# A sparse attention kernel with a mixture of depths: three kinds of small VectorE operations put behind a maximum, ScalarE's copies of the softmax sums left out, and one tile's gate product two maxima later

## The chip, the core and the metric

The kernel runs on one core of a Trainium2 chip. The core has five engines that run their own instruction streams side by side and wait for each other through semaphores: TensorE (PE in the profile; PEld are its weight loads), VectorE (DVE), ScalarE (ACT), GpSimd (POOL) and SyncE (SP), which here only starts DMAs. The metric is the device time of one execution in microseconds, as a median over runs.

## The reference

Two blocks, one after the other. `B, H, S, D` = 8, 8, 576, 64.

```python
scores = scale * np.matmul(q, k.transpose(0, 1, 3, 2))
kth = np.partition(scores, -32, axis=-1)[..., -32:-31]
scores = np.where(scores >= kth, scores, -1e9)
attn = np.exp(scores - np.max(scores, axis=-1, keepdims=True))
attn = attn / (np.sum(attn, axis=-1, keepdims=True) + 1e-09)
x = np.matmul(attn, v)                      # heads side by side: (B, S, 512)

gates = np.einsum('bsd,d->bs', x, w_gate)
out = x.copy()
for b in range(B):
    top = np.argpartition(-gates[b], 128)[:128]
    ye = np.maximum(x[b, top] @ w1, 0.0) @ w2
    out[b, top] = x[b, top] + ye / (1 + np.exp(-gates[b, top]))[:, None]
```

Each row of 576 scores keeps its 32 largest. Each batch then sends its 128 tokens with the largest gates through two matrix products.

## The kernel before

**Tiles and units.** The 576 query rows of a batch are four full tiles of 128 rows and a fifth of 64. A unit is two heads of a full tile (or four heads of the short one), so that a batch has 4 x 4 + 2 = 18 units and the whole run 144. A loop over `n` takes the units through a pipeline: in iteration `n` the scores of unit `n+1` are multiplied and copied to SBUF (`sc`), unit `n` gets a bound for its 32nd largest score, unit `n-1` is split at the bound, unit `n-2` gets its exact 32nd largest score (`kth_of`), unit `n-3` is masked and unit `n-4` is transposed, exponentiated and multiplied with `v`. All engines issue in the order in which the program is written.

**VectorE's share of a unit.** `find_bound`: for each of two rows of heads seven maxima over a seventh of the scores each (`cand<-sc`, 14 in a unit; one MAX8 instruction gives the eight largest), then rounds of maxima and replacements on these candidates. `find_kth`: two long maxima (`next<-y`), the last big instructions of a unit. Between these stand small ones. `find_bound` empties a list `vector_late` ahead of the second seven maxima; and `amid_late` holds the gate product of one tile with the number of the maximum in front of which it goes in the second seven.

**GpSimd's share.** For each unit two products (`y<-sc,sides`), a short `fill` of `y`, and one half of the mask (`less<-sc,next`); for each tile of queries the division by the softmax sums (`x<-xs,rden`); besides this the choice of the mixture's rows and its gathers and scatters.

**A tile's end.** When the last unit of a tile of queries has been multiplied with `v`, ScalarE copies the result into `xs` (eight heads of 64 columns and one column with the sum). `keep_sums` copies the eight sums into the constant tile `sums`, adding 1e-9. In the next iteration `normalise` takes the reciprocal on VectorE (`rden<-sums`, from `vector_late`) and has GpSimd multiply (`x<-xs,rden`). One iteration later `gates` takes the product of `x` with the gate's weights on VectorE (`prod<-x,wg`, a two-input operation with an accumulator). In the second seven maxima it stands in front of the maximum 2 in the first, fourth and fifth tile, 4 in the second and third.

**The mixture of a batch** is a generator, whose steps `mix_at` places in units of the batch that follows. Of its small VectorE operations three kinds matter here:
- `add_up`, run from `after_kth` behind `find_kth`: `add_parts` sums up a place (`place<-places`), `keep_rows` makes the row index (`row_i<-place`), then `g` is limited from below, and an `Exp` of `g` is put into `late`, a list for ScalarE that is emptied once in each iteration.
- `squash`, from `vector_late`: `g` plus 1, and its reciprocal.
- `keep_least`, at the end of each batch: the least of all 32nd largest scores (`least<-next`), for a check at the end of the kernel.

At the end of the kernel a list of such checks is worked off (two of them on `sums`), and if one fails, a slow general path runs. The last units stand outside the loop, written out by hand, with `sums_of` for the last two tiles.

Of the kernel before, what the change touches and what calls it, by code (L numbers as in the profile page):

```python
# [49 lines left out]
def kernel(  # L50
# [91 lines left out]
    seen = const.tile([P, NS], FP32, name="seen")  # L142
    least = const.tile([P, B], FP32, name="least")
    bounded = const.tile([P, NS], FP32, name="bounded")
    sums = const.tile([P, B * NT, H], FP32, name="sums")
    nc.gpsimd.memset(sums, 1.0)

    MIDDLE = S - 2 * (TOP_K - 8) + 1
    steps_i = const.tile([P, 2, 8], I32, name="steps_i")
# [74 lines left out]

    kept, values_bank = [], [None]

    after_kth = []

    def flush_copies():
        while copies_late:  # L230
# [14 lines left out]

    def flush_all():
        flush_vector()
        flush()
        flush_pool()

# [293 lines left out]
    def find_bound(sc, bound):  # L544

        cand = wkpool.tile([P, 2, 8 * PARTS], FP32, name="cand")
        best = [stats.tile([P, 2, 8], FP32, name=f"best{r}") for r in range(2)]
        best.append(bound)
        for i in range(2):

            if i == 1:
                flush_vector()
            for u in range(PARTS):
                if i == 1 and amid_late and u == amid_late[0][0]:
                    amid_late.pop()[1]()
                dve.max(
                    cand[:, i, 8 * u : 8 * u + 8],
                    sc[:, i, u * S // PARTS : (u + 1) * S // PARTS],
                )


        parts = cand.rearrange("p i (u e) -> p i u e", u=PARTS)
        for r, e in enumerate((3, 7, 8)):
            for i in range(2):
                dve.max(best[r][:, i, :], parts[:, i, :, 0:e])
            if r < 2:
                for i in range(2):
                    dve.match_replace(
                        parts[:, i, :, 0:e],
                        best[r][:, i, :],  # L570
                        parts[:, i, :, 0:e],
                        LOWEST,
                    )
# [140 lines left out]
    def keep_values_of_two(t, g, av, xs):  # L714
# [7 lines left out]
        for i, (h, r) in enumerate(heads_of(t, g)[0]):  # L722
# [4 lines left out]
                in_=both[r : r + n, :].rearrange("p (g c) -> p g c", g=2),  # L727
            )

    def normalise(b, t, xs):  # L730
        n = R if t == J else P
        den = sums[0:n, b * NT + t, :]
        divide(n, xs, of_batch[b][0][0:n, t, :], den)

    def keep_sums(n, xs, den):
        act.activation(den, xs[0:n, :, D], AF.Copy, bias=1e-9)

    def divide(n, xs, x, den):
        rden = stats.tile([P, H], FP32, name="rden")
        dve.reciprocal(out=rden[0:n, :], in_=den)  # L740
        pool.tensor_tensor(
            x.rearrange("p (h d) -> p h d", h=H),
            xs[0:n, :, 0:D],
            rden[0:n, :].unsqueeze(2).to_broadcast([n, H, D]),
            ALU.mult,
        )

# [38 lines left out]
    def mixture(row0, pg, rank, exact=False, sign_sum=None):  # L786
# [107 lines left out]

        def add_up():
            add_parts(place, found)
            keep_rows(
                place,
                row_i,
                row0 if isinstance(row0, float) else row0[:, 0:1],  # L900
                float(done * S - 1),
            )
            dve.tensor_scalar_max(out=g, in0=place[:, 1:2], scalar1=-88.0)
            late.append(lambda: act.activation(g, g, AF.Exp, scale=-1.0))

        def squash():
            dve.tensor_scalar_add(out=g, in0=g, scalar1=1.0)
            dve.reciprocal(out=g, in_=g)

        kept.append(lambda: after_kth.append(add_up))  # L910
        if exact:
            for todo in (kept, after_kth):
                while todo:
                    todo.pop(0)()
        yield
# [126 lines left out]
    def gates(b, t):  # L1042
        dot_tile(t, *of_batch[b])
# [130 lines left out]
    def keep_least(b, bound, kth):  # L1174
        at = 2 * per_batch * b
        late.append(
            lambda: act.copy(
                out=bounded[:, at : at + 2 * per_batch].rearrange("p (n i) -> p n i", i=2),
                in_=bound,
            )  # L1180
        )
        dve.tensor_reduce(
            out=least[:, b : b + 1], in_=kth, axis=mybir.AxisListType.XY, op=ALU.min
        )

    def mask_of(n, on=None):
# [5 lines left out]
    for n in range(-1, N):  # L1192
# [35 lines left out]
            normalised = None  # L1228
        if gating is not None:

            amid_late.append((4 if gating[1] in (1, 2) else 2, lambda a=gating: gates(*a)))

# [47 lines left out]
        if is_unit(n - 4):  # L1282
            b4, t4, g4 = units[n - 4]
            values(t4, g4, pT, last, av, qkv[b4][2], 2 * DE * second)
            if n in place_steps:
                values_bank[0] = av
                next(mixtures[place_steps[n]])
                pieces[place_steps[n]] += 1
            if g4 == 0:
                xs = xpool.tile([P, H, DE], FP32, name="xs")  # L1290
                if t4 == 0:
                    x = xpool.tile([P, NT, HD], FP32, name="x")
                    pg = gates_of[b4 % 2]
                    of_batch[b4] = x, pg
            if second:
                keep_values_of_two(t4, g4 - 1, av, xs)
            if g4 == groups(t4) - 1:
                inverting = b4, t4, xs
                n4 = R if t4 == J else P
                keep_sums(n4, xs, sums[0:n4, b4 * NT + t4, :])  # L1300
            while kept:
                kept.pop(0)()

# [64 lines left out]
        b, t, g = units[m]  # L1368
        keep_values(t, g, weighed[m][3], xs)

    def sums_of(t, xs):
        n = R if t == J else P
        keep_sums(n, xs, sums[0:n, (B - 1) * NT + t, :])

    def mask_both(m):
        b, i = divmod(m, per_batch)
        masks[m] = wkpool.tile([P, 2, S], BF16, name="less")
# [45 lines left out]
    values_unit(N - 3)  # L1423
    weighed[N - 2][2]()
    keep_unit(N - 3, xs)
    sums_of(J - 1, xs)
    mask_both(N - 1)
    normalise(B - 1, J - 1, xs)
    store_full(last_out, x)
# [13 lines left out]
    for _ in range(2):  # L1443
        next(between)
    keep_unit(N - 1, xs)
    sums_of(J, xs)
    count(J - 1, slice(0, JP), rank)
    rden = stats.tile([P, H], FP32, name="rden")
    dve.reciprocal(out=rden[0:R, :], in_=sums[0:R, (B - 1) * NT + J, :])
    dve.tensor_tensor(  # L1450
        x[0:R, J, :].rearrange("p (h d) -> p h d", h=H),
        xs[0:R, :, 0:D],
        rden[0:R, :].unsqueeze(2).to_broadcast([R, H, D]),
        ALU.mult,
    )
    store_last(last_out, x)
# [77 lines left out]
        )  # L1534

    keep_least(B - 1, bounds.pop(B - 1)[:, :, :, 7], next8s.pop(B - 1)[:, :, :, 7])
    flush()
    low = modpool.tile([P, S], I32, name="low", tag="scratch")[:, 0:NS]
    dve.tensor_scalar(
# [9 lines left out]
    for what, op, than, limit in (  # L1549
        (bounded, ALU.min, ALU.is_gt, LEAST),  # L1550
        (least, ALU.min, ALU.is_gt, LEAST),
        (low, ALU.min, ALU.is_gt, 0.5),
        (seen, ALU.max, ALU.is_lt, float(MIDDLE)),
        (seen, ALU.min, ALU.is_gt, float(MIDDLE - 16)),
        (sums.rearrange("p t h -> p (t h)"), ALU.min, ALU.is_gt, FEWEST),
        (sums.rearrange("p t h -> p (t h)"), ALU.max, ALU.is_lt, MOST),
        (places[:, :, 6], ALU.min, ALU.is_gt, 0.5),
        (places[:, :, 6], ALU.max, ALU.is_lt, 1.5),
    ):
        far = stats.tile([P, 1], FP32, name="far", bufs=2)  # L1560
        dve.tensor_reduce(out=far, in_=what, axis=mybir.AxisListType.X, op=op)
        dve.scalar_tensor_tensor(
            out=sure, in0=far, scalar=limit, in1=sure, op0=than, op1=ALU.mult
        )
# [91 lines left out]
    def general(b, row0):  # L1656
        def of(a):
            return a[bass.ds(b, 1)].rearrange("o a s d -> (o a) s d")

        kT, qT, vs = room_for_qkv(0)  # L1660
        rows = Rows(of(k), of(q), kT, qT)
        turn_all_last(rows)
        for hp in range(NHP):
            turn_pair(rows, hp)
        load_v(of(v), vs)
        x = xpool.tile([P, NT, HD], FP32, name="x")
        pg = gates_of[0]
        for t in range(NT):
            xs = xpool.tile([P, H, DE], FP32, name="xs")
            for g in range(groups(t)):  # L1670
                ps = room_for_scores()
                multiply(t, g, kT, qT, by_head(ps))
                p = general_weights(keep(ps))
                tr, av = room_to_turn()
                turn(p, tr)
                pT = ptpool.tile([P, 2, J, P], FP32, name="pT")
                last = ptpool.tile([P, P], FP32, name="last")
                nc.scalar.copy(out=pT, in_=tr)
                nc.scalar.copy(out=last, in_=turn_last(p, av))
                values(t, g, pT, last, av, vs)  # L1680
                keep_values(t, g, av, xs)
            rows = R if t == J else P
            den = stats.tile([P, H], FP32, name="den", bufs=1)
            keep_sums(rows, xs, den[0:rows, :])
            divide(rows, xs, x[0:rows, t, :], den[0:rows, :])
            dot_tile(t, x, pg)
        store(out[bass.ds(b, 1)].rearrange("o s n -> (o s) n"), x)
        rank = stats.tile([P, NT], FP32, name="rank", bufs=1)
        for _ in mixture(row0, pg, rank, exact=True):
            flush_all()  # L1690
        flush_all()
# [40 lines left out]
```

## Time and profile before

| | us |
|---|---|
| median of 3 runs | 787.77 (785.72 to 788.05) |
| the profiled execution | 788.09 |
| its span in the profile | 785.8 |
| busy: PE, PEld | 725.5, 550.6 |
| busy: DVE | 755.1 |
| busy: ACT | 731.7 |
| busy: POOL | 693.7 |

The profiler shows the span of the engines' work; the execution's own time has 2.3 us around it. An engine's busy time is the time that at least one of its instructions was under way. Instructions of one engine can overlap in the profile[...]. What an instruction costs its engine is therefore read from one start to the next rather than from its duration. A row that gives a count merges instructions that follow each other, with the time from the first one's start to the last one's end.

The groups of instructions that the change touches, all at line 46 (a helper that records every operation), with count, mean duration of one, and the idle time of the engine in front of them:

| engine, operation | count | mean ns | idle before, us |
|---|---|---|---|
| DVE maximum `cand<-sc`, 82 columns | 1440 | 228 | 4.6 |
| DVE maximum `next<-y` | 288 | 751 | 0.0 |
| DVE product `prod<-x,wg`, 128 rows | 32 | 794 | 0.1 |
| DVE reciprocal `rden<-sums`, 128 rows | 32 | 185 | 1.4 |
| DVE reduction `least<-next` | 8 | 217 | 0.2 |
| DVE reduction `place<-places` | 7 | 141 | 0.0 |
| DVE `row_i<-place` | 8 | 154 | 0.3 |
| DVE `g<-g`, plus 1 | 8 | 133 | 0.3 |
| DVE reciprocal `g<-g` | 8 | 164 | 0.3 |
| ACT copy `sums<-xs`, 128 rows | 32 | 216 | 1.0 |
| POOL mask `less<-sc,next` | 135 | 1731 | 24.6 |

### The profile page before, as it was taken

To read this page: it belongs to the slowest core of one execution; us is meant where nothing else is said; L and a number is where in the kernel's file an instruction comes from. 1 tells how busy PE (TensorE), PEld (TensorE's weight loads), DVE (VectorE), ACT (ScalarE), POOL (GpSimd) and SP (SyncE) were. 2 spreads that over 40 slices of the span, in tenths; PEclk is the share of its full clock that TensorE was granted. 3 is DMA by queue.
4 is the path that set the end of the run, shared out by engine and by line. 5 is a ranking of instruction groups with operands and counts; after the bars stand their busy time and mean duration, and the time that the engine had idled before them with its cause. 6 is when DMAs were issued, how large, how long until landed. Compare 5 with 4: busy or idle time off the path is not lost. (4 is left out here: it accounts for less than half of the span.)

```text
span 785.8 us, 33176 instructions
## 1 busy us (share of the span) xinstructions
PE 725.5 (92%) x12535; PEld 550.6 (70%) x12535; DVE 755.1 (96%) x4602; ACT 731.7 (93%) x1535; POOL 693.7 (88%) x732
## 2 busy tenths in 40 slices
PE   8888888788999989999999999999899999999987
PEld 6666666566786668766787667866687668757756
DVE  6999999999999999999999999999999999999952
ACT  5999999999999999999999999999999999989830
POOL 3899999999999999999999999999999999899821
PEclk9999999999999999999999999999999999999999
DMA  9941214121151223321232221412234102101021
GB/s 171 297 86 35 58 62 104 36 56 30 62 113 25 52 66 76 83 55 37 77 89 52 56 43 62 105 30 56 43 89 92 30 15 70 25 15 17 3 75 31
DMA packets 121751, 50.69 MB, mean 65 GB/s; under 512 B 116016, under 2 KB 116016, under 8 KB 120560
## 3 DMA queue, kind: packets, MB, share of 16 engines
q1 hardware_dynamic: 118368, 43.94, 22.9%
q0 software_dynamic: 1744, 4.20, 3.0%
q8 instruction: 101, 1.65, 0.9%
q14 instruction: 66, 0.54, 0.3%
q10 hardware_dynamic: 1472, 0.36, 0.2%
HBM read 36.93 MB, written 11.55 MB: 62 GB/s over the span
## 5 line engine op out<-in xcount | busy, mean ns | idle before, releaser
L46 POOL TENSOR_TENSOR y<-sc,sides 128x576 f32<-128x576 f32 x288 | 350.5, 1240 | 27.9 <-ACT sides L46 26.2
L46 DVE MAX8 cand<-sc 128x8 f32<-128x82 f32 (+1 forms) x2016 | 312.8, 228 | 4.6 <-ACT sc L46 4.6
L46 POOL TENSOR_SCALAR less<-sc,next 128x576 bf16<-128x576 f32 x135 | 233.7, 1731 | 24.6 <-DVE next L46 21.9
L46 ACT ACTIVATE sides<-sc,bound 128x576 fp8e4<-128x576 f32 x288 | 230.9, 802 | 2.1 <-DVE bound L46 1.5
L46 PEld LDWEIGHTS av<-v,pT 128*64 128x64 f32 x4608 | 146.9, 138 | 87.5 <-ACT last L46 79.0
L46 DVE MAX8 next<-y 128x8 f32<-128x584 f32 x288 | 204.4, 751 | 0.0
L46 PE MATMUL av<-v,pT 128*64 128x65 f32 x4608 | 166.9, 225 | 35.2 <-ACT last L46 34.9
L46 PE MATMUL ps<-kT,qT 64*128 64x288 f32 (+1 forms) x1248 | 170.4, 422 | 3.2 <-ACT sc L46 2.5
L46 PEld LDWEIGHTS <-less 64*128 64x128 bf16 (+1 forms) x2448 | 160.6, 131 | 11.2 <-POOL less L46 8.3
L46 ACT COPY sc<-ps 128x1152 f32<-128x1152 f32 x140 | 160.7, 1148 | 0.0
L46 PE MATMUL ptr<-ident,sc 64*128 64x64 f32 x2272 | 160.1, 252 | 0.0
L46 ACT ACTIVATE pT<-ptr 128x1024 f32<-128x1024 f32 x142 | 147.4, 1038 | 9.4 <-PE ptr L46 8.7
L46 PEld LDWEIGHTS ptr<-ident,sc 64*128 64x128 f32 x2272 | 137.6, 137 | 23.8 <-issue 23.6
L46 PE MATMUL ptr<-out_of_reach,less 64*128 64x64 bf16 x2272 | 147.1, 189 | 5.6 <-POOL less L46 4.9
L46 ACT ACTIVATE less<-sc,next 128x576 bf16<-128x576 f32 x147 | 115.5, 790 | 0.0
L46 PEld LDWEIGHTS ps<-kT,qT 64*128 64x128 f32 (+1 forms) x1248 | 92.6, 176 | 22.8 <-ACT sc L46 5.6
L46 DVE MATCH_REPLACE8 cand<-best,cand 128x21 f32<-128x21 f32 (+1 forms) x576 | 99.0, 180 | 0.0
L46 DVE MAX8 best<-cand 128x8 f32<-128x21 f32 (+1 forms) x576 | 90.6, 190 | 0.0
L46 ACT ACTIVATION_READ_ACCUMULATOR sides<-sc,bound 128x1 f32 x288 | 63.8, 222 | 0.0
L46 PE MATMUL h_ps<-xeT,w 128*128 128x128 f32 x464 | 61.9, 278 | 0.0
L46 PEld LDWEIGHTS av<-ident,sc 128*128 128x128 f32 x144 | 20.0, 139 | 55.9 <-issue 40.9
L46 PE MATMUL av<-vpair,last 128*64 128x130 f32 x576 | 56.9, 276 | 0.0
(167 smaller groups left out, 919.0 us busy)
## 6 DMA issues: line engine op xcount, KB each, us to landing
v<-in_v_dram SPq DMA_DIRECT2D x64, 128.0 KB, 4.0
out_dram<-x SPq DMA_DIRECT2D x8, 1024.0 KB, 3.9
rows<-in_k_dram SPq DMA_DIRECT2D x56, 128.0 KB, 3.0
rows<-in_q_dram SPq DMA_DIRECT2D x56, 128.0 KB, 3.0
w<-in_moe_w_dram SPq DMA_DIRECT2D x2, 2048.0 KB
gate_row<-row_dram SPq DMA_DIRECT2D x7, 288.0 KB, 4.4
last<-in_q_dram SPq DMA_DIRECT2D x8, 128.0 KB, 3.4
vpair<-in_v_dram SPq DMA_DIRECT2D x16, 64.0 KB, 5.1
```

The source lines that it names most:

```text
L46: return lambda *a, **kw: self._tc.keep_in_program_order(fn(*a, **kw))
```

## The change

A new list `after_max` is emptied by `flush_small` behind every one of the 14 maxima of `find_bound`. Into it go the reduction for `least`, the row index and the limit of `g` with the `Exp` behind it (now `use_place`; the sum `add_parts` stays where it was), and the reciprocal in `squash`. Each of these therefore stands behind the first maximum that is issued after the operation that put it there. Because `use_place` runs after its iteration's `late` list has been emptied, the `Exp` of `g` comes one iteration later on ScalarE.

`keep_sums` and `sums_of` are gone: the reciprocal reads column 64 of each head of `xs` and writes into a constant tile `shares`, which the multiplication reads. The 1e-9 isn't added any more, and the checks at the end look at `shares` with inverted limits.

The gate product of the second tile stands in front of maximum 6 instead of 4.

```diff
+    after_kth, after_max = [], []
+
+    def flush_small():
+        while after_max:
+            after_max.pop(0)()
...
                     sc[:, i, u * S // PARTS : (u + 1) * S // PARTS],
                 )
+                flush_small()
...
     def normalise(b, t, xs):
         n = R if t == J else P
-        den = sums[0:n, b * NT + t, :]
-        divide(n, xs, of_batch[b][0][0:n, t, :], den)
-
-    def keep_sums(n, xs, den):
-        act.activation(den, xs[0:n, :, D], AF.Copy, bias=1e-9)
-
-    def divide(n, xs, x, den):
-        rden = stats.tile([P, H], FP32, name="rden")
-        dve.reciprocal(out=rden[0:n, :], in_=den)
+        invert(xs[0:n, :, D], share_of(b, t))
+        divide(n, xs, of_batch[b][0][0:n, t, :], share_of(b, t))
+
+    def invert(den, share):
+        dve.reciprocal(out=share, in_=den)
...
         def add_up():
             add_parts(place, found)
+            after_max.append(use_place)
+
+        def use_place():
             keep_rows(
...
             dve.tensor_scalar_add(out=g, in0=g, scalar1=1.0)
-            dve.reciprocal(out=g, in_=g)
+            after_max.append(lambda: dve.reciprocal(out=g, in_=g))
...
-        dve.tensor_reduce(
-            out=least[:, b : b + 1], in_=kth, axis=mybir.AxisListType.XY, op=ALU.min
+        after_max.append(
+            lambda: dve.tensor_reduce(
+                out=least[:, b : b + 1], in_=kth, axis=mybir.AxisListType.XY, op=ALU.min
+            )
         )
...
-            amid_late.append((4 if gating[1] in (1, 2) else 2, lambda a=gating: gates(*a)))
+            amid_late.append(((2, 6, 4, 2, 2)[gating[1]], lambda a=gating: gates(*a)))
...
-                n4 = R if t4 == J else P
-                keep_sums(n4, xs, sums[0:n4, b4 * NT + t4, :])
...
     keep_unit(N - 1, xs)
-    sums_of(J, xs)
     count(J - 1, slice(0, JP), rank)
-    rden = stats.tile([P, H], FP32, name="rden")
-    dve.reciprocal(out=rden[0:R, :], in_=sums[0:R, (B - 1) * NT + J, :])
+    invert(xs[0:R, :, D], share_of(B - 1, J))
```

More of the change, by code (lines that the diff above doesn't have):

```diff
@@ L144 @@
     bounded = const.tile([P, NS], FP32, name="bounded")
-    sums = const.tile([P, B * NT, H], FP32, name="sums")
-    nc.gpsimd.memset(sums, 1.0)
+    shares = const.tile([P, B * NT, H], FP32, name="shares")
+    nc.gpsimd.memset(shares, 1.0)
     MIDDLE = S - 2 * (TOP_K - 8) + 1
@@ L225 @@
     kept, values_bank = [], [None]
-    after_kth = []
+    after_kth, after_max = [], []
+    def flush_small():
+        while after_max:
+            after_max.pop(0)()
     def flush_copies():
@@ L559, in find_bound @@
                 )
+                flush_small()
         parts = cand.rearrange("p i (u e) -> p i u e", u=PARTS)
@@ L728, in keep_values_of_two, with share_of, divide @@
             )
+    def share_of(b, t):
+        return shares[0 : R if t == J else P, b * NT + t, :]
     def normalise(b, t, xs):
         n = R if t == J else P
-        den = sums[0:n, b * NT + t, :]
-        divide(n, xs, of_batch[b][0][0:n, t, :], den)
-    def keep_sums(n, xs, den):
-        act.activation(den, xs[0:n, :, D], AF.Copy, bias=1e-9)
-    def divide(n, xs, x, den):
-        rden = stats.tile([P, H], FP32, name="rden")
-        dve.reciprocal(out=rden[0:n, :], in_=den)
+        invert(xs[0:n, :, D], share_of(b, t))
+        divide(n, xs, of_batch[b][0][0:n, t, :], share_of(b, t))
+    def invert(den, share):
+        dve.reciprocal(out=share, in_=den)
+    def divide(n, xs, x, share):
         pool.tensor_tensor(
@@ L743, in divide @@
             xs[0:n, :, 0:D],
-            rden[0:n, :].unsqueeze(2).to_broadcast([n, H, D]),
+            share.unsqueeze(2).to_broadcast([n, H, D]),
             ALU.mult,
@@ L907, in squash @@
             dve.tensor_scalar_add(out=g, in0=g, scalar1=1.0)
-            dve.reciprocal(out=g, in_=g)
+            after_max.append(lambda: dve.reciprocal(out=g, in_=g))
         kept.append(lambda: after_kth.append(add_up))
         if exact:
-            for todo in (kept, after_kth):
+            for todo in (kept, after_kth, after_max):
                 while todo:
@@ L1369, in keep_unit @@
         keep_values(t, g, weighed[m][3], xs)
-    def sums_of(t, xs):
-        n = R if t == J else P
-        keep_sums(n, xs, sums[0:n, (B - 1) * NT + t, :])
     def mask_both(m):
@@ L1425 @@
     keep_unit(N - 3, xs)
-    sums_of(J - 1, xs)
     mask_both(N - 1)
@@ L1452 @@
         xs[0:R, :, 0:D],
-        rden[0:R, :].unsqueeze(2).to_broadcast([R, H, D]),
+        share_of(B - 1, J).unsqueeze(2).to_broadcast([R, H, D]),
         ALU.mult,
@@ L1536 @@
     keep_least(B - 1, bounds.pop(B - 1)[:, :, :, 7], next8s.pop(B - 1)[:, :, :, 7])
+    flush_small()
     flush()
@@ L1554 @@
         (seen, ALU.min, ALU.is_gt, float(MIDDLE - 16)),
-        (sums.rearrange("p t h -> p (t h)"), ALU.min, ALU.is_gt, FEWEST),
-        (sums.rearrange("p t h -> p (t h)"), ALU.max, ALU.is_lt, MOST),
+        (shares.rearrange("p t h -> p (t h)"), ALU.max, ALU.is_lt, 1.0 / FEWEST),
+        (shares.rearrange("p t h -> p (t h)"), ALU.min, ALU.is_gt, 1.0 / MOST),
         (places[:, :, 6], ALU.min, ALU.is_gt, 0.5),
@@ L1682, in general @@
             rows = R if t == J else P
-            den = stats.tile([P, H], FP32, name="den", bufs=1)
-            keep_sums(rows, xs, den[0:rows, :])
-            divide(rows, xs, x[0:rows, t, :], den[0:rows, :])
+            den = stats.tile([P, H], FP32, name="den", bufs=1)[0:rows, :]
+            act.activation(den, xs[0:rows, :, D], AF.Copy, bias=1e-9)
+            invert(den, den)
+            divide(rows, xs, x[0:rows, t, :], den)
             dot_tile(t, x, pg)
```

## The prediction

> **What bounds the kernel now.** I read the busy time of each engine by stretches first, then VectorE's waits, then VectorE's timeline, where the start times matter more than the durations. One stretch from the middle (columns: stretch, length, busy time of TensorE's matmuls, its weight loads, VectorE, ScalarE, GpSimd; granted clock; DMA share; GB/s):
>
> ```profile
> 450.00:540.00 90.00, 86.55 (x1514) 65.62 (x1513) 89.90 (x560) 89.25 (x188) 85.16 (x88) 1.00 0.27 63
> ```
>
> VectorE is busy 89.90 of 90 us, ScalarE 89.25. Only one of two such engines can set the pace, and the waits tell which: in the whole table VectorE waits for a score copy (`cand` for `sc`) three times, 4.6 us together, all in the first 45 us, and for `sums` twice, 2.4 us, both in the last 36 us. In between its stream is closed: every instruction that takes less room moves all that follows. ScalarE does wait, little (`pT` for TensorE 8.7 us, `sides` for VectorE's bound 1.5 us). So between 45 and 749 us the sum is made on VectorE alone; from 749 us, where VectorE starts to wait, it is a chain through all engines.
>
> What is an instruction's room? VectorE's timeline (start, length, engine, line, operation, tiles, count):
>
> ```profile
> 181.68 0.75 DVE L46 MAX8 next<-y 128x8 f32<-128x584 f32 x1
> 182.34 0.14 DVE L46 TENSOR_REDUCE place<-places 128x2 f32<-128x6 f32 x1
> 182.52 0.15 DVE L46 TENSOR_SCALAR row_i<-place 128x1 int32<-128x1 f32 x1
> 182.59 0.14 DVE L46 TENSOR_SCALAR g<-place 128x1 f32<-128x1 f32 x1
> 182.65 0.38 DVE L46 MAX8 cand<-sc 128x8 f32<-128x82 f32 x2
> ...
> 196.82 0.75 DVE L46 MAX8 next<-y 128x8 f32<-128x584 f32 x1
> 197.61 0.22 DVE L46 TENSOR_REDUCE least<-next 128x1 f32<-128x36 f32 x1
> 197.74 0.38 DVE L46 MAX8 cand<-sc 128x8 f32<-128x82 f32 x2
> ...
> 203.57 0.13 DVE L46 TENSOR_SCALAR g<-g 128x1 f32<-128x1 f32 x1
> 203.74 0.16 DVE L46 RECIPROCAL g<-g 128x1 f32<-128x1 f32 x1
> ...
> 314.59 0.75 DVE L46 MAX8 next<-y 128x8 f32<-128x584 f32 x1
> 315.26 0.81 DVE L46 MAX8 cand<-sc 128x8 f32<-128x82 f32 x5
> ```
>
> The last two rows are the plain case: the second `next` lasts 0.75 us, but the maximum behind it starts after 0.67. Five `cand` maxima of 0.228 us take 0.81, so they start every 0.145. An instruction that needs nothing of its predecessor starts 0.08 us before that one ends. `least` reads `next`: it starts 0.79 after it, 0.035 past its end. A dependence thus costs 0.12 us of VectorE each time, and the profile books it as busy.
>
> **The small operations, part by part.** All three kinds occur once in each of 7 batches inside the closed stretch.
> 1. `least` goes from straight behind `next` to behind the next unit's first maximum. `next` to successor: 0.79 becomes 0.67; `least`'s own 0.13 stays. Gain 0.12.
> 2. `place` stays; `row_i` and `g` go behind the maximum. `place` to `row_i` is 0.18 now; to a maximum that doesn't read it, 0.14 - 0.08 = 0.06. When `row_i`'s turn comes, 0.06 + 0.15 = 0.21 us after `place` began, its operand (ready at 0.18) is there. One maximum more stands behind a one-element operation and takes 0.153 instead of 0.145. Gain 0.11.
> 3. `squash`: the addition to its reciprocal takes 0.17 now, 0.13 - 0.08 = 0.05 with a maximum between. Gain 0.11, once 0.09 (one addition, at 659.4 us, lasts 0.10 behind a `rden`).
>
> Sum: 7 x (0.12 + 0.11 + 0.11) - 0.02 = **2.36 us**.
>
> A rule speaks against this. The Trainium skill, "VectorE: DVE Perf Modes", section "The DRAIN you can't avoid", says that a Vector operation does not start until the pipeline behind the last one is empty, with or without semaphores, and its rules for authors conclude that one should lower the count of operations, not the waits. By that the reorder gains 0, for the count is the same (the section adds that an operation which is not held starts earlier). The rows 314.59 and 196.82 have the same predecessor and differ by 0.12 us, so I take the row: 2.36.
>
> What the move delays: `row_i` comes some 0.2 us later in the unit; the gather that needs it stands on GpSimd behind a `less` and starts 2.3 us into that unit, so it doesn't notice. ScalarE's `Exp` of `g` is queued a whole unit later (4.7 us); the addition that reads it comes four units or more after `place`, so 5 us or more stay.
>
> **No copies of sums.** 40 ScalarE activations of 0.216 us go. They also wait for the copy of `xs` in front: `xs` to `sums` takes 0.446 from start to start, `xs` to anything else 0.256, and 0.12 behind `sums`: 0.31 us each, 12.5 us of ScalarE in all. In the closed stretch that is worth 0 on VectorE, which never waits for ScalarE there. It is cover, though: with VectorE 0.4 us a batch faster and ScalarE idle some 0.7 per 90, ScalarE would have come near to the bound. Built, the changed program has 36 more `sc` copies that name a second wait; 95 have it today without an idle row in front, so 0.
>
> The reciprocal now reads `xs` with a stride of 65 elements. No row shows it on VectorE; the nearest, a reduction over 8 elements seven apart, lasts 160 ns, over 8 adjacent ones 154: between 0 and 40 x 0.006 = 0.24 us. I take 0, the eight elements being so few.
>
> In the tail the copy is on the path:
>
> ```profile
> 754.29 0.54 ACT L46 COPY xs<-av 64x130 f32<-64x130 f32 x2 [1.02 <-PE av L46]
> 754.86 0.21 ACT L46 ACTIVATE sums<-xs 64x8 f32<-64x8 f32 x1
> ```
>
> VectorE has been idle for 1.05 us when `rden` starts at 755.11; `xs` is complete at 754.83. The reciprocal can start at 754.87: **0.24 us**, and everything behind (`x`, the gate, its transposition, counts, gather) is serial. The same for the tile before (750.31) is worth nothing: GpSimd's `x` and the gate behind it are done before VectorE's wait for `xs` at 754.
>
> **The product of the gates.** VectorE's two-input product takes 0.60 us to its accumulator's read where nothing disturbs it, but not in the second tile (GpSimd's row first, then VectorE's):
>
> ```profile
> 438.58 1.74 POOL L46 TENSOR_SCALAR less<-sc,next 128x576 bf16<-128x576 f32 x1
> ...
> 439.13 0.76 DVE L46 CUSTOM_DVE_ANT_0 prod<-x,wg 128x512 f32<-128x512 f32 x1
> 439.82 0.08 DVE L46 DVE_READ_ACCUMULATOR2_ANT gate<- 128x1 f32 x1
> ```
>
> 0.69 here. Over all 40: a product that starts 0.36 us after a `less` takes 0.87 to 0.90, at 0.54 it takes 0.68 to 0.73, at 0.58 0.64, from 0.66 on 0.60. So only the first 0.62 us or so of a `less` hold the product up. The second tile loses 129, 121, 92, 84, 83 and 80 ns in six batches and nothing in the first two. Two maxima later is 0.29 us later, some 0.83 behind `less`: the loss goes. Gain **0.59 us**; `less` outlasts the product (0.83 + 0.60 < 1.69), so the `y` behind it isn't met.
>
> Here too a rule differs: "SBUF — State Buffer", section "Who interferes with whom", has a two-input Vector operation blocked by a GpSimd operation that reads SBUF until that one finishes. By it the product at 439.13 should have taken 1.2 + 0.6 us; the row has 0.69. By the rule the move would still wait for the end of `less`, but 0.29 less, 8 x 0.29 = 2.3 us. I take the row's 0.59; the 2.3 sets the low end.
>
> The other tiles: the third starts 1.18 behind its `less` and comes 0.11 nearer, no loss. The fourth starts 0.98 behind; `least` and `squash` bring it 0.23 nearer, and the moved `Exp` may push ScalarE, and so GpSimd, another 0.11 back: about 0.65, right at the edge, a loss of 0 to 0.03 per batch; I take 0.
>
> **Sum.** 2.36 + 0.59 + 0.24 = 3.19 us. The profiled execution took 788.09 (span 785.8 and 2.3 around it) and would take 784.9; it lies 0.3 above the median of the three runs, 787.77, so the forecast for a median is **784.6**.
>
> **Rivals.**
> - *The pipeline empties anyway.* Only 0.59 + 0.24 remain: 786.9. For it: the rule; against it: the two `next` rows. Chance 0.08.
> - *GpSimd falls back against a faster VectorE.* Products of the first, fourth and fifth tile (now 0.36, 0.98, 0.58 behind `less`) meet `less` about 0.1 us earlier: 7 x 0.3 = 2.1 us back, 786.7. Against it: `less` waits for `next` 38 times, which re-aligns GpSimd several times a batch. Chance 0.12.
> - *The moved product meets `y`.* If GpSimd runs so far ahead that `less` is over, the second tile's product stands behind a `y` of 1.21 us: 8 x 1.2 - 2.6 = 7 us slower, 794.8. It decides once GpSimd is 0.86 us earlier than in the row; ScalarE's relief before that unit is one copy, 0.31. Chance 0.04.
> - *ScalarE sets the pace after all*: up to 12.5 us go, 775. VectorE's closed stream speaks against it. Chance 0.02.
>
> Forecast 0.74. About 0.3% (2.4 us, below 785.4) is what a measurement tells from no change; the forecast lies only 0.8 beyond it and the three runs spread over 2.3 us, so of its 0.74 I put 0.08 into "same". Faster 0.66 + 0.04 + 0.02 = 0.72, same 0.08 + 0.08 + 0.08 = 0.24, slower 0.04. The range runs from the rule's 2.3 us for the product (782.9) to the second rival (786.7).
>
> **What would show it.** `next` to its successor 0.67 in every unit, no step of 0.17 behind `place` or `g`; the second tile's products at 0.60; `xs` to reciprocal under 0.1 us in the tail; VectorE without idle rows between 45 and 745 us. I am wrong if the fourth tile's product grows past 0.60, if VectorE waits for `sc` or `y`, or if the reciprocal's room exceeds today's 0.10.

## The result and the profile after

The changed kernel takes 782.7 us (median of 7 runs, 782.27 to 784.74) against 787.59 us (median of 7, 784.96 to 788.05); the ratio is 0.9955, with a 95% interval of 0.994 to 0.997, so about 3.5 us less. The two medians are further apart than that, 4.9 us, because they fall into different groups of runs some 2 us apart: in seven of the twelve profiles of this document the first maximum of unit 4 starts at 25.4 to 25.8 us, in five at 27.3 to 27.5, VectorE having waited longer for its first score copies (4.6 us against 2.9 in one profile of each). The profiled executions of the kernel before and of the changed one, in both of which unit 4 starts late, took 788.09 and 784.74: 3.35 us less.

The page of the kernel after, busy time of each engine:

```profile
PE 726.4 (93%) x12535; PEld 551.1 (70%) x12535; DVE 752.6 (96%) x4602; ACT 724.4 (93%) x1495; POOL 692.6 (89%) x732
```

and the same middle stretch as in the prediction, with the same columns:

```profile
450.00:540.00 90.00, 86.97 (x1517) 65.50 (x1511) 90.00 (x556) 88.87 (x184) 84.86 (x87) 1.00 0.26 63
```

VectorE is now busy without any rest. ScalarE's busy time fell only from 89.25 to 88.87, although it lost 0.216 us five times a batch: a batch is shorter now, and ScalarE's other instructions last longer on average (a score copy 1161 ns instead of 1148, `sides` 814 instead of 802). Why they do is not shown; ScalarE's share alone says little here.

VectorE's timeline of the kernel after, at the three kinds of small operations (start, length, engine, line, operation, tiles, count):

```profile
182.33 0.14 DVE L46 TENSOR_REDUCE place<-places 128x2 f32<-128x6 f32 x1
182.39 0.23 DVE L46 MAX8 cand<-sc 128x8 f32<-128x82 f32 x1
182.54 0.13 DVE L46 TENSOR_SCALAR row_i<-place 128x1 int32<-128x1 f32 x1
182.59 0.14 DVE L46 TENSOR_SCALAR g<-place 128x1 f32<-128x1 f32 x1
...
197.34 0.23 DVE L46 MAX8 cand<-sc 128x8 f32<-128x82 f32 x1
197.48 0.20 DVE L46 TENSOR_REDUCE least<-next 128x1 f32<-128x36 f32 x1
197.60 0.52 DVE L46 MAX8 cand<-sc 128x8 f32<-128x82 f32 x3
...
203.29 0.13 DVE L46 TENSOR_SCALAR g<-g 128x1 f32<-128x1 f32 x1
203.34 0.23 DVE L46 MAX8 cand<-sc 128x8 f32<-128x82 f32 x1
203.50 0.14 DVE L46 RECIPROCAL g<-g 128x1 f32<-128x1 f32 x1
```

The successor of `place` and that of the addition to `g` start about 0.08 us before the end of the one in front; the steps of 0.17 to 0.18 us behind them are 0.06 and 0.05 now. Besides, the moved operation itself takes less room: `least` needs 0.117 us to the next start instead of 0.134, `row_i` 0.052 instead of 0.071, the reciprocal of `g` 0.061 instead of 0.080. With its neighbours, `least` gains 0.135 us, `place` 0.128, `squash` 0.128.

The second tile's product, in the same batch as in the prediction (GpSimd's row, then VectorE's two):

```profile
436.94 1.72 POOL L46 TENSOR_SCALAR less<-sc,next 128x576 bf16<-128x576 f32 x1
...
437.98 0.67 DVE L46 CUSTOM_DVE_ANT_0 prod<-x,wg 128x512 f32<-128x512 f32 x1
438.58 0.08 DVE L46 DVE_READ_ACCUMULATOR2_ANT gate<- 128x1 f32 x1
```

It takes 0.60 us to its accumulator's read. It starts 1.04 us behind the start of the mask (called the mask's lead below), though, where 0.54 + 0.29 = 0.83 was forecast: the mask itself has moved 0.21 us forward against VectorE. That is the first sign that the parts of the change are not independent.

The tail, VectorE's timeline: the end of the last mask (the read of its accumulator) and the last two reciprocals. Before:

```profile
748.84 0.09 DVE L46 DVE_READ_ACCUMULATOR less<-sc,next 128x1 f32 x1
750.31 0.20 DVE L46 RECIPROCAL rden<-sums 128x8 f32<-128x8 f32 x1 [1.38 <-ACT sums L46]
...
755.11 0.20 DVE L46 RECIPROCAL rden<-sums 64x8 f32<-64x8 f32 x1 [1.05 <-ACT sums L46]
```

After:

```profile
745.72 0.08 DVE L46 DVE_READ_ACCUMULATOR less<-sc,next 128x1 f32 x1
746.95 0.20 DVE L46 RECIPROCAL shares<-xs 128x8 f32<-128x8 f32 x1 [1.14 <-ACT xs L46]
...
751.51 0.20 DVE L46 RECIPROCAL shares<-xs 64x8 f32<-64x8 f32 x1 [0.57 <-ACT xs L46]
```

VectorE's last mask ended at 748.93 us before and ends at 745.80 now. From there to the last reciprocal it was 6.18 us and is 5.70: the tail gained 0.48 us, twice the forecast. (TensorE's granted clock, which is halved once for 3.4 us here and changes the tail, falls 5.08 us ahead of the end of the last mask in the one profile and 5.05 in the other, so that the two can be compared.)

Put together, in the profiled executions: from unit 4 to the last mask 3.27 us less, the tail to the last reciprocal 0.48 less, the stretch ahead of unit 4 0.15 more, what follows the last reciprocal 0.25 more: some 3.35. The causes of the last two are not shown.

### The profile page after: what moved, and what is told of

It reads as the page before. It is cut to its first block, busy times and chain, and to the rows that moved or that the text cites. A ratio compares the mean times of both kernels' runs of the same rounds, so it can differ in the third digit from the quotient of the medians.

```text
span 782.5 us, 33174 instructions
## 1 busy us (share of the span) xinstructions
PE 726.4 (93%) x12535; PEld 551.1 (70%) x12535; DVE 752.6 (96%) x4602; ACT 724.4 (93%) x1495; POOL 692.6 (89%) x732
## 5 line engine op out<-in xcount | busy, mean ns | idle before, releaser
L46 ACT ACTIVATE sides<-sc,bound 128x576 fp8e4<-128x576 f32 x288 | 234.5, 814 | 4.4 <-DVE bound L46 4.3
L46 ACT COPY sc<-ps 128x1152 f32<-128x1152 f32 x140 | 162.5, 1161 | 0.0
L46 PE MATMUL ptr<-ident,sc 64*128 64x64 f32 x2272 | 161.8, 252 | 0.0
L46 ACT ACTIVATE pT<-ptr 128x1024 f32<-128x1024 f32 x142 | 150.0, 1056 | 11.8 <-PE ptr L46 10.4
L46 ACT ACTIVATE less<-sc,next 128x576 bf16<-128x576 f32 x147 | 117.2, 801 | 0.0
L46 ACT ACTIVATION_READ_ACCUMULATOR sides<-sc,bound 128x1 f32 x288 | 67.3, 234 | 0.0
```

Of the source, the lines that this page charges most:

```text
L46: return lambda *a, **kw: self._tc.keep_in_program_order(fn(*a, **kw))
```

## The experiments

Three numbers are read from each profile, all in us: the loop (from the first maximum of unit 4 to the end of the last mask on VectorE), the length of a middle batch (from the first maximum of batch 4 to that of batch 5, counted from 0), and the excess of VectorE's two-input products over 0.599 us (start to the accumulator's read), added up over the 8 batches for each of the five tiles. VectorE has no idle row within the loop of any of them. The tail has its own part below.

| kernel | ratio to before (95%) | loop | batch | excess of products, tiles 1 to 5 |
|---|---|---|---|---|
| before | | 721.60 | 92.09 | 3.30, 0.59, 0, 0.02, 0.26 |
| after | 0.9955 (0.994 to 0.997) | 718.32 | 91.58 | 3.19, 0, 0, 0.11, 0.23 |
| small operations only | 0.9978 (0.9966 to 0.9989) | 719.64 | 91.89 | 2.27, 0.04, 0, 2.30, 0.22 |
| without copies only | 0.9987 (0.9972 to 1.0001) | 720.88 | 91.97 | 2.98, 0, 0, 0.02, 0.18 |
| product at 6 only | 0.9996 (0.9983 to 1.001) | 720.81 | 91.98 | 3.06, 0, 0, 0.02, 0.26 |
| after, product at 4 | 0.9958 (0.9944 to 0.9971) | 718.32 | 91.58 | 3.14, 0, 0, 0.09, 0.19 |
| small only, fourth tile at 6 | 0.9978 (0.9968 to 0.9987) | 720.44 | 91.91 | 3.63, 1.00, 0, 0.76, 0.19 |
| after, first tile at 5 | 0.9927 (0.9908 to 0.9946) | 716.01 | 91.32 | 0.63, 0.26, 0, 0.10, 0.02 |
| after, unread copies | 0.9965 (0.9949 to 0.9981) | 719.27 | 91.77 | 1.82, 2.16, 0, 0.10, 0.20 |
| first tile at 5, unread copies | 0.9949 (0.9931 to 0.9966) | 718.66 | 91.76 | 1.78, 1.66, 0.19, 0.12, 0.02 |

### The small operations alone

```diff
 kernel before
+                flush_small()
...
+            after_max.append(use_place)
...
+            after_max.append(lambda: dve.reciprocal(out=g, in_=g))
...
+        after_max.append(lambda: dve.tensor_reduce(out=least[:, b : b + 1], ...
```

> The kernel before with the small operations behind a maximum and nothing else (copies of sums kept, second tile's product in front of maximum 4). Measure: the end of VectorE's last mask in the profile, 748.93 us before and 745.80 with the whole change. Theory (each dependence costs 0.12 us, and a small operation gets another 0.02 us shorter behind a maximum): 7 x 0.39 = 2.7 us earlier, 746.2; ratio about 0.9965. The prediction's sizes: 2.4 us, 746.6. Rival (the pipeline empties behind each operation anyway): 748.9, ratio 1.000. If ScalarE becomes the pace with its copies kept, VectorE shows idle rows in front of cand and the gain is under 2 us.

The loop is 1.95 us shorter, not 2.7 and not 0. The steps on VectorE behave as they do in the changed kernel, so the rival that the pipeline empties behind every operation is ruled out here. No idle row stands in front of `cand` in the loop either. What went lost is in the fourth tile's product, 1.15 us long in four batches (2.3 us more, while the first and second tiles' products lose 1.6 us less). GpSimd's timeline and VectorE's in one of them:

```profile
384.93 1.71 POOL L46 TENSOR_SCALAR less<-sc,next 128x576 bf16<-128x576 f32 x1
...
384.98 1.23 DVE L46 CUSTOM_DVE_ANT_0 prod<-x,wg 128x512 f32<-128x512 f32 x1
386.14 0.08 DVE L46 DVE_READ_ACCUMULATOR2_ANT gate<- 128x1 f32 x1
```

The mask starts 0.05 us ahead of the product, and the product gets through only 0.61 us after the mask's start. In the kernel before, the same mask had a lead of 0.98 us. And where the two start together, as in the first tile of the same kernel, or the product up to 0.12 us ahead, as in the second, GpSimd is the one that is held up; the first tile:

```profile
415.34 2.27 POOL L46 TENSOR_SCALAR less<-sc,next 128x576 bf16<-128x576 f32 x1
...
415.34 0.68 DVE L46 CUSTOM_DVE_ANT_0 prod<-x,wg 128x512 f32<-128x512 f32 x1
415.94 0.09 DVE L46 DVE_READ_ACCUMULATOR2_ANT gate<- 128x1 f32 x1
```

The mask takes 2.27 us instead of 1.72. So with the copies kept, GpSimd's masks come late against the faster VectorE. The waits say who makes them late: between 360 and 630 us GpSimd waits 6.4 us for ScalarE's `sides` (4.0 before, 2.8 after) and only 2.7 for VectorE's `next` (8.0 before, 9.5 after).

### Without the copies alone

```diff
 kernel before
-                keep_sums(n4, xs, sums[0:n4, b4 * NT + t4, :])
...
-    sums_of(J - 1, xs)
...
-    sums_of(J, xs)
...
+        invert(xs[0:n, :, D], share_of(b, t))
```

> The kernel before without the copies of sums and nothing else. Theory: VectorE never waits for ScalarE in the loop, but GpSimd's masks in the second tile's unit start about 0.2 us earlier against VectorE, so that the product in front of maximum 4 starts about 0.75 us behind its mask and takes 0.60 as well: the last mask ends 0.5 us earlier, less 0.2 for the strided reciprocals (each makes the maximum behind it 0.005 longer): 748.6. In the tail both reciprocals count, 0.48 us: from the last mask to the last reciprocal 5.70 us instead of 6.18. In all about 0.8 us faster, ratio 0.999. The prediction's view: loop 748.9 and tail 0.24, ratio 0.9997.

The loop is 0.72 us shorter, more than the 0.3 expected: the second tile's product loses nothing at its old place, and the first tile's, which was expected to stay, loses 0.3 less. From the last mask to the first of the two reciprocals this profile can't be compared: the granted clock was 0.51 over 740 to 747 us, twice as long as in most of the others. From the first reciprocal to the last it is 4.56 us, as in the changed kernel. That both reciprocals count was tested by itself, below.

### The changed kernel with the product back at 4

```diff
-            amid_late.append(((2, 6, 4, 2, 2)[gating[1]], lambda a=gating: gates(*a)))
+            amid_late.append(((2, 4, 4, 2, 2)[gating[1]], lambda a=gating: gates(*a)))
```

> The changed kernel with the second tile's product back in front of maximum 4. Theory: once the copies of sums are gone the mask starts early enough, the product starts about 0.75 us behind it and takes 0.60: no loss, the last mask ends at 745.8 as in the changed kernel. The prediction's view (the later place is what saves 0.59 us): 746.4.

The second tile, GpSimd's row, then VectorE's two:

```profile
434.95 1.74 POOL L46 TENSOR_SCALAR less<-sc,next 128x576 bf16<-128x576 f32 x1
...
435.72 0.67 DVE L46 CUSTOM_DVE_ANT_0 prod<-x,wg 128x512 f32<-128x512 f32 x1
436.32 0.08 DVE L46 DVE_READ_ACCUMULATOR2_ANT gate<- 128x1 f32 x1
```

The mask's lead is 0.77 us, where it was 0.55 in the kernel before, and the product takes 0.60. The loop is the same within 0.01 us. The later place contributes nothing once the copies are gone.

### The product at 6 alone

The same line, in the kernel before.

> The kernel before with the second tile's product in front of maximum 6 and nothing else. Theory and prediction alike: all eight products of the second tile take 0.60 us, the last mask ends 0.59 us earlier, 748.3; ratio about 0.9993. Rival (a two-input operation waits for the end of the mask): the product takes 1.4 us or more.

All eight products of the second tile take 0.60 us, as both views had it, and the first tile's lose 0.25 less as well; the loop is 0.78 us shorter. None of the eight waited for the end of its mask.

### Small operations alone, the fourth tile's product at 6

```diff
 small operations only
-            amid_late.append((4 if gating[1] in (1, 2) else 2, lambda a=gating: gates(*a)))
+            amid_late.append(((2, 4, 4, 6, 2)[gating[1]], lambda a=gating: gates(*a)))
```

> The kernel with the small operations alone behind a maximum (copies of sums kept), the fourth tile's product in front of maximum 6 instead of 2. In that kernel ScalarE comes too late for GpSimd, the mask in the fourth tile's unit starts just before the product, and the product takes 1.15 us in four batches. Theory: four maxima are 0.58 us, the product then starts 0.63 us behind the mask and takes 0.60 to 0.62: from unit 4 to the last mask 717.5 us instead of 719.6. Rival (the 2 us come from something else that ScalarE delays, such as waits for sc): stays at 719.6.

A miss. The fourth tile's excess fell from 2.30 to 0.76, but the first and second tiles' products lost 2.3 us more, and the loop grew by 0.8 (0.7 of it in the last batch). What one product no longer loses, others lose: in batches 3 to 6 the first two tiles' products start 0.8 to 1.0 us behind a `y` on GpSimd, which holds them up until 1.1 us after its start. The middle batch shows it: 91.91 us here and 91.89 before the edit. That suggests that something else fixes the length of a batch and the products only adapt to it. With the copies kept, ScalarE is the candidate.

### Copies that nobody reads

```diff
 kernel after (and: first tile at 5)
                 inverting = b4, t4, xs
...
+                act.activation(unread[0:n4, :], xs[0:n4, :, D], AF.Copy, bias=1e-9)
```

> The changed kernel with ScalarE's copies of the sums back at every tile's end in the loop, into a tile that nothing reads; the reciprocals still read xs. Theory (with its copies ScalarE has too much work for a batch and sets the pace, through GpSimd's masks and the products behind them): the middle batches take 91.9 us as in both kernels with the small operations alone, instead of 91.6, and some products stand behind a fresh mask again; from unit 4 to the last mask about 719.7 us instead of 718.3. Rival (what counts is the chain from xs through the copy to the reciprocal, which is shorter now): 91.6, 718.3.

> The kernel with the first tile's products in front of maximum 5 (91.33 us for a middle batch), with the same unread copies. Theory: ScalarE's work for a batch does not care where VectorE's products stand, so again 91.9 us, 0.3 more than the changed kernel although VectorE has less to do. Rival (ScalarE only shifts the masks by a fixed amount): products that start 0.8 us behind their masks keep 0.60, 91.4 us or less.

A middle batch is as long in the one as in the other, 91.77 and 91.76 us, though without the copies the second kernel takes 91.32 and the first 91.58. The copies are work for ScalarE alone, nothing waits for what they write, and they set the same length for two different arrangements of VectorE's work. The products show how VectorE is held back without one idle row. The second tile with unread copies, GpSimd's row, then VectorE's:

```profile
435.72 1.76 POOL L46 TENSOR_SCALAR less<-sc,next 128x576 bf16<-128x576 f32 x1
...
435.98 1.06 DVE L46 CUSTOM_DVE_ANT_0 prod<-x,wg 128x512 f32<-128x512 f32 x1
436.97 0.08 DVE L46 DVE_READ_ACCUMULATOR2_ANT gate<- 128x1 f32 x1
```

The mask's lead is 0.26 us where the changed kernel has 1.04, and the product takes 0.99. Read together with the waits: ScalarE's work for a batch, copies included, fills about 91.8 us; a faster VectorE runs ahead of it until its products meet fresh masks, which GpSimd comes to late because it waits for ScalarE's `sides` (5.0 and 6.7 us between 360 and 630 us in these two kernels, 2.8 in the changed one). ScalarE in turn waits 1.8 us for VectorE's bound between 270 and 630 us in the changed kernel and has no such wait in these two (nor in the kernel before). The level is 0.1 us lower than the expected 91.9, which was that of the kernels in which the reciprocals read the copies; that difference is left open.

### The tail, copy by copy

```diff
 kernel after
+    den = stats.tile([P, H], FP32, name="den", bufs=1)
+    act.activation(den, xs[:, :, D], AF.Copy, bias=1e-9)
...
-    normalise(B - 1, J - 1, xs)
+    invert(den, share_of(B - 1, J - 1))
+    divide(P, xs, x[:, J - 1, :], share_of(B - 1, J - 1))
```

and a second kernel that does the same for the last short tile too.

> The changed kernel with ScalarE's copy of the sums back for the last full tile of the last batch alone. Theory (its reciprocal, GpSimd's x and the gate's product release a transposition that stands in TensorE's queue in front of the last unit's values): the last mask to that reciprocal 1.38 us instead of 1.14, and to the last reciprocal 5.93 instead of 5.70. The prediction's view (worth nothing): the last reciprocal stays at 5.70.

> The changed kernel with ScalarE's copies of the sums back for the last full tile and the last short tile of the last batch. Theory: both delays add up, the last mask to the last reciprocal 6.18 us as in the kernel before. The prediction's view: 5.94.

With one copy back, VectorE's timeline:

```profile
747.39 0.20 DVE L46 RECIPROCAL shares<-den 128x8 f32<-128x8 f32 x1 [1.39 <-ACT den L46]
...
751.95 0.20 DVE L46 RECIPROCAL shares<-xs 64x8 f32<-64x8 f32 x1 [0.80 <-ACT xs L46]
```

Its last mask ended at 746.00: the first reciprocal comes 1.39 us behind it (1.14 without the copy), the last 5.94 (5.70). The second reciprocal was not touched, and follows the first at 4.55 us, as in the changed kernel (4.56). With both back the distance between the two is 4.80, as before (4.81). From the last mask to the last reciprocal it is 6.01, against the 6.18 expected and the 5.94 of the other view, for the first one comes at 1.21 there. That first distance moves with the halving of the clock, which starts 5.90 us ahead of the last mask's end here and 5.08 in the kernel before; it is the part of this test that stays unclean. Ratios to the kernel before: 0.9971 (0.9961 to 0.998) and 0.9973 (0.9965 to 0.9981).

Why the first counts, TensorE's timeline shows. The changed kernel:

```profile
747.90 1.15 PE L46 MATMUL av<-v,pT 128*64 128x65 f32 x32
748.88 0.39 PE L46 MATMUL av<-vpair,last 128*64 128x130 f32 x4
749.29 0.29 PE L46 MATMUL ptr<-ident,gate 128*128 128x128 f32 x1
749.51 1.15 PE L46 MATMUL av<-v,pT 128*64 128x65 f32 x32
```

With one copy back:

```profile
748.10 1.16 PE L46 MATMUL av<-v,pT 128*64 128x65 f32 x32
749.09 0.39 PE L46 MATMUL av<-vpair,last 128*64 128x130 f32 x4
749.73 0.29 PE L46 MATMUL ptr<-ident,gate 128*128 128x128 f32 x1 [0.25 <-DVE gate L46]
```

The gate's transposition, which needs the product behind that reciprocal, stands in TensorE's queue ahead of the last unit's multiplication with `v`, which the last `xs` comes from. With the copy, TensorE stands idle for 0.25 us until the gate is there, and everything behind is as much later: the transposition starts 1.63 us behind the multiplication in the first row instead of 1.39, and the last reciprocal follows it by 2.22 us in both.

### The first tile's product at 5

```diff
 kernel after
-            amid_late.append(((2, 6, 4, 2, 2)[gating[1]], lambda a=gating: gates(*a)))
+            amid_late.append(((5, 6, 4, 2, 3)[gating[1]], lambda a=gating: gates(*a)))
```

> The changed kernel with the products of the first tile in front of maximum 5 instead of 2 and of the fifth in front of 3 instead of 2. Theory (only the first 0.62 us of a mask hold the product up; the first tile's product starts 0.36 us behind its mask, 3 maxima are 0.44 us): the six products of batches 1 to 6 take 0.60 instead of 0.86 to 0.88, the fifth tile's 0.60 instead of 0.63, those of batches 0 and 7 lose some 0.4 us less each. From the first maximum of unit 4 to the end of the last mask 715.6 to 716.4 us instead of 718.3; ratio to the kernel before about 0.9925. Rival (blocked for the whole mask): the first tile's product still ends with the mask, a gain of 0.44 at most each, but then it would have to take 0.9 us or more.

The line also moves the fifth tile's product from 2 to 3. The first tile's product in the changed kernel, GpSimd's row, then VectorE's:

```profile
416.42 1.72 POOL L46 TENSOR_SCALAR less<-sc,next 128x576 bf16<-128x576 f32 x1
...
416.76 0.93 DVE L46 CUSTOM_DVE_ANT_0 prod<-x,wg 128x512 f32<-128x512 f32 x1
417.63 0.07 DVE L46 DVE_READ_ACCUMULATOR2_ANT gate<- 128x1 f32 x1
```

And with the product at 5:

```profile
415.13 1.75 POOL L46 TENSOR_SCALAR less<-sc,next 128x576 bf16<-128x576 f32 x1
...
415.94 0.68 DVE L46 CUSTOM_DVE_ANT_0 prod<-x,wg 128x512 f32<-128x512 f32 x1
416.54 0.09 DVE L46 DVE_READ_ACCUMULATOR2_ANT gate<- 128x1 f32 x1
```

The product starts 0.81 us behind its mask instead of 0.35 and takes 0.60 instead of 0.87, and ends well before the mask. The loop takes 716.01 us, as expected, 2.3 less than in the changed kernel; the ratio to the kernel before is 0.9927, the time 780.32 us (median of 6, 778.51 to 782.02). Of what the first two tiles still lose, 0.56 and 0.26 us fall in the last batch.

## Why the prediction was right, and where it was not

The forecast, faster and by 3.19 us, holds: 3.35 are between the two profiles, and the ratio of 0.9955 on the 787.77 us from which it was made gives 784.2 against 784.6. The median itself, 782.7, lies 0.2 us under the low end of the range, because the forecast was made from runs whose first score copies mostly came later. But two steps of the prediction failed, and one part was credited with a gain that another part gives as well. That the sum stayed so close is luck in part: the small operations and the tail gained 0.4 and 0.24 us more than forecast, and about 0.5 went elsewhere, most of it ahead of the loop and behind the last reciprocal.

- **The small operations** (2.36 us): the mechanism is right. The mis-sized term is the moved operation's own room, taken as unchanged; it shrinks by 0.02 us, so that a batch gains 0.39 us instead of 0.34 on these steps, 2.7 us in all.
- **The rule against it**, that the pipeline empties behind each operation, doesn't hold in these profiles: `place` to a maximum takes 0.058 us, to `row_i` 0.175.
- **"In the closed stretch that is worth 0 on VectorE"**, of the copies: this step failed. VectorE never waits for ScalarE in any idle row of that stretch, but it is held up by it through GpSimd: a late `sides` makes a late mask, and a late mask holds up a product, which the profile books as VectorE's work. In the four kernels with a faster VectorE that kept the copies in the loop, a middle batch took 91.76 to 91.91 us however the products stood, and the small operations alone gave 1.95 of their 2.7 us. The prediction called the time that the copies free on ScalarE a cover, and had ScalarE come near to the bound without it; the cover was needed.
- **The product's later place** (0.59 us): the second tile's loss is gone as forecast, but in the changed kernel the place isn't the cause. At 4 the loop is the same, since without the copies the mask starts 0.2 us earlier. Either alone suffices, as the two kernels with one of them each show.
- **The rule that a product waits for its mask's end**: not seen. Products of 128 rows that start 0.63 us or more behind a mask took 0.60 in all twelve profiles, with the mask still running.
- **The tail** (0.24 us): right for the last reciprocal. "The same for the tile before (750.31) is worth nothing" failed: it is worth another 0.24. The prediction asked when VectorE has to wait next, and not what stands behind the gate in TensorE's queue.
- **The fourth tile at the edge** (0 to 0.03 us a batch): its product starts 0.63 us behind the mask in four batches and loses nothing; in batch 1 (counted from 0), 0.53 behind, it lost 0.09. That is one of the prediction's signs of being wrong, come true once and small.
- **The strided reciprocal**: taken as 0 with a bound of 0.24. The maximum behind it takes 0.116 us to the next start instead of 0.112, and it itself 0.102 instead of 0.101: over 38 tiles 0.19 us.
- **The rivals**: the moved product never stood behind a `y`, and GpSimd's falling back and ScalarE's pace, put at chances of 0.12 and 0.02, don't hold for the changed kernel but are just what the small operations alone run into.

## What to carry to other kernels

Read start to start rather than durations: a dependent operation directly behind its operand cost a gap of about 0.12 us here that the profile books as busy, and one independent instruction between them took it away. An engine without idle rows can still be paced by another one, when a third engine, made late by that one, holds it up in the middle of an instruction: if two arrangements of its work give the same length of a period, look for the engine whose work doesn't change. Before moving an instruction out of a stall, ask whether another part of the change moves what it collides with.

## What the runs showed of the hardware that was not expected

- A mask on GpSimd and a two-input product on VectorE hold each other up, but not for the whole mask: a mask of 1.72 us holds the product up only until 0.61 to 0.68 us after the mask's start; a product of 0.60 us that is first, or starts up to 0.05 us behind the mask, makes the mask last 2.15 to 2.28 us. For products of 128 rows the turn lies at a lead of about 0.05 us: at 0.045 the product was first, at 0.050 the mask.
- A small operation takes 0.02 us less to the next start behind a maximum that it doesn't read than directly behind its operand (`least` 0.117 instead of 0.134). The reason is not shown.
- In nine of the twelve profiles the granted clock is halved once for 3.4 us shortly before the last mask (0.59 on average over 740.0 to 744.2 us in the changed kernel). The two profiles in which this lasted 6.8 us have the longest tails (last mask to the last `place` 12.5 and 13.0 us, 11.5 in the changed kernel), and the one without it, the changed kernel with unread copies, the shortest (10.2). These differences are larger than the tail's whole gain, so a tail is compared only where the halving lies alike, or from one reciprocal to the next: that step is 4.80 us in the five profiles whose last reciprocal reads a copy and 4.55 to 4.56 in the seven others, wherever the halving lies.
